# Projection products of the last sections as two row halves, with one ring of seven PSUM banks

## The chip, the cores and the metric

The kernel runs on one core of a Trainium2 chip. Five engines work side by side, each through its own queue in order: TensorE (PE) multiplies matrices into PSUM, VectorE (DVE) and ScalarE (ACT) read PSUM, GpSimd (POOL) works on SBUF, and SyncE (SP) issues most DMAs. PSUM has eight banks; one holds a tile of 128 partitions by 512 fp32. The metric is the device time of one execution in microseconds, the median over several runs.

## The reference, cut to what matters

Two branches of one input x (2048 tokens, 512 features) are mixed by a gate per token:

```python
g = sigmoid((x * gate_w).sum(-1))
a = Re(DFT_seq(DFT_hidden(x)))                 # four matrix products with cos/sin matrices
q, k, v = heads(x @ wqkv)                      # 32 heads of 16
p = softmax(q @ k.T * 16 ** -0.5)              # full 2048 x 2048 per head
b = concat_heads(p @ v) @ wo                   # the projection
out = g * a + (1 - g) * b
```

The change concerns the projection with `wo` and the scores of the last head pair.

## The kernel before, in words

Matrix products keep fp32 accuracy by splitting an operand into a high and a low part of a reduced fp32 type: one product becomes three, high x high, high x low, low x high.

Heads are worked in 16 pairs. For a pair p, the 2048 queries are taken in two halves of 1024, and the keys in 16 tiles of 128: a *unit* u is one pair, one half and one key tile, 512 units in all. In a unit, `scores` makes four score tiles (two query blocks, two heads), each with the keys of 128 positions as stationary operand and 512 queries moving. Head 0 lies on rows 0 to 49 of the operands and head 1 on rows 64 to 113, so the scores of the two heads use different row halves of the PE array. Fifty rows hold the three split products and the row of maxima that makes the exponent safe. The maxima come from a second, transposed score tile (`a_tile`) that DVE reduces. ACT takes the exponential of each score tile from PSUM into `pt` (line 775); four value products per unit (`pv`, `pv_last`), each in its own 32 columns of the array, add into the bank `acc`.

Most of the kernel interleaves, by patterns written out by hand, one score or maximum on one row half with one product of the Fourier branch or the projection on the other row half (`segment`). When the maxima are done, the last ten *sections*, the loop at line 994, follow: u = 492, 494, to 510, two units each. A section issues, in this order on PE, four scores (two starts of two), the projection products that the table `whole` gives it, four more scores, and the eight value products of two earlier units (16 records in the profile). In 506, `turn` follows the products: four small products with the matrix `pairsum`, by which the last pair's sums and outputs are turned. In 508 `back`, one transpose, follows them. Both use all 128 rows.

A projection *chain* (`Chain`) is the sum of several products of 128 rows for one output tile t of 128 tokens in one PSUM bank: nine products over the head blocks 0 to 2 (generator `first`), or three for one block (`third`, `last`, `early`). When a chain's last product is issued, `proj_next` calls `finish`, which has DVE compute y = y + (1 - g) * PSUM (line 649) and, for the last block of the first token half, sends y out.

The eight banks are: `acc`; `psD` ("d") with one bank; and six banks in two rings of three, `psS` ("s", banks 0 to 2) and `psA` ("a", banks 3 to 5). A ring gives the bank that was touched least recently; a tile's first product waits until the last reader of the tile before it in that bank is done. In the last sections the scores of head 0 use ring s, those of head 1 ring a. Chains use d and s in turn, in 508 and 510 a, d and s. Ahead of section 492 stand four extra scores of head 1, in banks s, s, a and d.

After the sections, `products` makes the last pair's own projection for four output tiles, then come the last value products and `last_pair` with the end of the work.

Of the kernel before, what the change touches and what calls it, by code (L numbers as in the profile page):

```python
# [9 lines left out]
F32 = mybir.dt.float32  # L10
# [5 lines left out]
P = 128  # L16
# [15 lines left out]
def mix_kernel(ctx: ExitStack, tc: tile.TileContext, xa_t, xa, wqkv, w_hid, w_seq, wo, gate_w, out):  # L32
# [5 lines left out]
    nc = tc.nc  # L38
    ctx.enter_context(tc.manual_schedule())

    six = [ctx.enter_context(tc.tile_pool(name=f"ps{i}", bufs=1, space=PSUM)) for i in range(6)]

    used = list(range(6))

    class Ring:


        def __init__(self, *banks):
            self.banks, self.of = banks, {}

        def tile(self, shape, dtype, name, bank=None):
            i = min(self.banks, key=used.index) if bank is None else bank
            t = six[i].tile(shape, dtype, name=name, tag="t")
            self.touch(i)
            self.of[id(t)] = (t, i)
            return t
# [7 lines left out]
            if id(t) in self.of:  # L64
                self.touch(self.of[id(t)][1])

    psS, psA = Ring(0, 1, 2), Ring(3, 4, 5)
    psO = ctx.enter_context(tc.tile_pool(name="psO", bufs=1, space=PSUM))
    psD = ctx.enter_context(tc.tile_pool(name="psD", bufs=1, space=PSUM))
    dram = ctx.enter_context(tc.tile_pool(name="dram", bufs=1, space=DRAM))  # L70
# [114 lines left out]
    def bank():  # L185
        nonlocal banks
        banks += 1
        return (psS if banks % 2 else psA).tile([P, 512], F32, name="s" if banks % 2 else "a")


    with tc.tile_pool(name="qk", bufs=1, reuse_waits="tile") as pool:
# [38 lines left out]
        for tb in range(4):  # L230
# [4 lines left out]
            for c in range(2):  # L235
                if tb == 0 and c == 0:
                    pss = [bank() for _ in range(4)]
                    for kt in range(KT):
                        x = xab[tb][:, :, :, kt * P:(kt + 1) * P]
                        for i, (w, v) in enumerate(((wh, 0), (wl, 0), (wh, 1))):  # L240
                            for ct in range(4):
                                nc.tensor.matmul(pss[ct], w[:, c, kt, ct * P:(ct + 1) * P], x[:, :, v],
                                                 start=kt == 0 and i == 0, stop=kt == KT - 1 and i == 2)
# [4 lines left out]
                for ct in range(4):  # L248
                    ps = bank()
# [143 lines left out]
    for s in range(8):  # L393
        ps = psS.tile([P, 512], F32, name="s")
# [45 lines left out]
    class Chain:  # L440


        def __init__(self, pool, name, n):
            self.pool, self.name, self.left = pool, name, n
            self.begun = False

        def mm(self, st, mv, half, stop):
            if not self.begun:
                self.ps = self.pool.tile([P, 512], F32, name=self.name)
            r = slice(None) if half is None else slice(64 * half, 64 * half + 64)  # L450
            i = nc.tensor.matmul(self.ps, st[r], mv[r], start=not self.begun, stop=stop)  # L451
            self.begun = True
            return i

    def real():

        for s, t in enumerate(ab):
            chain = Chain(*((psA, "a") if s in (0, 2) else (psD, "d")), 12)
            for kt in range(KT):
                h1, l1 = (t[:, v, kt * P:(kt + 1) * P] for v in range(2))  # L460
                yield chain, h1, wre[0][kt], None
                yield chain, h1, wre[1][kt], None
                yield chain, l1, wre[0][kt], partial(real_next, s, t, chain) if kt == KT - 1 else None
# [58 lines left out]
    oh, yp, wos = {}, {}, []  # L522
# [115 lines left out]
    maxima_left = True  # L638

    def finish(ps, t, y, other=False):  # L640
        for ring in (psS, psA):
            ring.read(ps)
        if other:

            tmp = few
            nc.scalar.activation(tmp, ps, AF.Copy, scale=omg[:, t:t + 1])  # L646
            nc.gpsimd.tensor_tensor(y, y, tmp, ALU.add)  # L647
            return
        nc.vector.scalar_tensor_tensor(y, ps, omg[:, t:t + 1], y, op0=ALU.mult, op1=ALU.add)

    def proj(hf, cts, pools, qts=range(8)):

        for qt in qts:
            t = hf * 8 + qt
            chain = Chain(*pools[qt % len(pools)], 3 * len(cts))
            for ct in cts:
                h1, l1 = oh[hf, ct][qt]
                for i, (st, mv) in enumerate(((h1, 0), (h1, 1), (l1, 0))):
                    last = ct == cts[-1] and i == 2
                    yield chain, st, wos[0][:, mv, ct], partial(proj_next, hf, cts, t, chain) if last else None  # L660

    def proj_next(hf, cts, t, chain):
        finish(chain.ps, t, yp[t], maxima_left)
        if hf == 0 and cts[-1] == 3:
            nc.sync.dma_start(out[t * P:(t + 1) * P, :], yp[t])

# [22 lines left out]
    class LastPair:  # L689
# [35 lines left out]
        def products(self, pools, order, others=()):  # L725

            pss = [pool.tile([P, 512], F32, name=name) for pool, name in pools]
            for i, (st, mv) in enumerate(((0, 0), (0, 1), (1, 0))):
                for c in range(4):
                    r = slice(32 * c, 32 * c + 32)  # L730
                    nc.tensor.matmul(pss[c], self.o15[r, st], w15[0][r, mv], start=i == 0, stop=i == 2)
            for c in order:
                t = 8 + 4 * self.blk + c
                y = yp.pop(t)
                finish(pss[c], t, y, c in others)
                (nc.scalar if c in others else nc.sync).dma_start(out[t * P:(t + 1) * P, :], y)
# [3 lines left out]
    def last_pair(fill):  # L740
        x = LastPair(1, [(psS, "s")])
        x.copy(4)
        pump(fill, 1)
        x.turn()
        pump(fill, 4)
        x.back()
        drain(fill)
        x.products([(psA, "a")] * 3 + [(psD, "d")], (1, 2, 0, 3), (0,))
# [12 lines left out]
    def scores(u, qb, h, bank=(psS, "s"), number=None):  # L761
        p, r = divmod(u, 32)
        hf, kt = divmod(r, 16)
        q0 = hf * 1024 + qb * 512
        if u >= UNITS - 16:

            blk, kt = divmod(kt, 8)
            q0, kt = 1024 + blk * 512, 2 * kt + qb
        if u not in pts:
            pts[u] = work.tile([P, 4, 512], F32, name="pt", bufs=4)  # L770
        pool, name = bank
        ps = pool.tile([P, 512], F32, name=name) if number is None else pool.tile([P, 512], F32, name, number)
        rr = slice(64 * h, 64 * h + 50)
        nc.tensor.matmul(ps, ks[p % 2][rr, kt * P:(kt + 1) * P], qs[p % 2][rr, q0:q0 + 512], start=True, stop=True)  # L774
        return nc.scalar.activation(pts[u][:, 2 * qb + h], ps, AF.Exp, bias=0.0, scale=DH ** -0.5)  # L775
# [33 lines left out]
    def take(gen, n, whole=True):  # L809

        got = []
        while len(got) < n:
            x = next(gen, None)
            if x is None:
                break
            x[0].left -= 1
            got.append((*x, x[0].left == 0))
            if whole and got[-1][4]:
                break
        return got  # L820

    def issue(x, half, stop=True):
        chain, st, mv, after, last = x
        i = chain.mm(st, mv, half, last and stop)
        if stop and after:
            after()
        return i

    def pump(gen, n):
        for x in take(gen, n, False):  # L830
            issue(x, None)

    def drain(gen):
        while xs := take(gen, 9):
            for x in xs:
                issue(x, None)
# [6 lines left out]
    for hf in range(2):  # L843
        for ct in range(4):
            n = 3 if hf and ct == 3 else 4
            last = 32 * (4 * ct + n - 1) + 16 * (hf + 1)
# [9 lines left out]
    one, two, three = [(psD, "d")], [(psS, "s"), (psD, "d")], [(psS, "s"), (psA, "a"), (psD, "d")]  # L856
# [9 lines left out]
    def run_plan(u):  # L866
        for v in sorted(v for v in plan if v <= u + 1):
            for f in plan.pop(v):
                f()
# [31 lines left out]
    def values(full=False):  # L901
        nonlocal valued
        i = pv(valued, full)
        valued += 1
        return i
# [56 lines left out]
    first = proj(0, (0, 1, 2), one * 5 + two[:1] + one, range(7))  # L962
# [21 lines left out]
    for bank in (*three[:1], *three):  # L984
# [3 lines left out]
    third = proj(1, (3,), two)  # L988
    last = proj(0, (3,), three[1:] + three[:1], range(7))

    early, late = proj(0, (0,), one, (7,)), proj(0, (1, 2, 3), [(psS, "s")], (7,))
    whole = {492: ((first, 9),), 494: ((first, 6),), 496: ((first, 3), (third, 3)), 498: ((third, 6),), 500: ((third, 6),),
             502: ((third, 3),), 504: ((early, 3), (third, 3)), 506: ((third, 3),), 508: ((last, 9),), 510: ((last, 12),)}
    for u in range(valued + 2, UNITS, 2):
        run_plan(u)
        for i in range(4):
            if i == 2:
                for gen, n in whole[u]:
                    pump(gen, n)
                if u == 506:  # L1000
                    last_pairs[0].turn()
                elif u == 508:
                    last_pairs[0].back()
            for h in range(2):
                scores(u + i // 2, i % 2, h, three[h])
        values()
        values()
    last_pairs[0].products([(psS, "s"), (psA, "a"), (psA, "a"), (psD, "d")], range(4))
# [39 lines left out]
```

## Time and profile before

| what | value |
|---|---|
| runs | 1698.32, 1698.53, 1698.54 us; median 1698.53 |
| span of the profiled execution, first to last instruction | 1696.8 us |
| busy share of the span | PE 100%, DVE 81%, ACT 67%, POOL 26% |
| the ten sections, first score of 492 to last value product of 510 | 1633.1 to 1683.4 us of the span |
| in 1633.1 to 1681.5 us | PE 48.4 busy, ACT 42.2, DVE 17.9 of 48.4 us |
| granted PE clock | 1.00 up to 1680 us |

The page gives the profiled execution's span and no other time for it. Rows of the timeline have the start in us from the span's start, the length in us, the engine, the source line, the operation, output<-input and shapes, the count of merged instructions, and in brackets the idle time before with what ended it. The end of a matrix product is modelled: its start is the surer number. Lengths of neighbouring products overlap, since they are pipelined.

### The profile page before, as it was taken

What the parts mean: (1) busy time and instruction counts of PE and PEld (TensorE: products, weight loads), DVE (VectorE), ACT (ScalarE), POOL (GpSimd) and SP (SyncE); (2) the same over time, 40 slices, a digit from 0 to 9 for tenths busy, and PEclk for the clock granted to TensorE, in tenths of its full rate; (3) what the DMA queues carried; (4) which work ended last, traced back from release to release, by engine and by line L of the source; (5) the groups of instructions that cost most, each with busy time, mean ns of one, the idle gap of its engine ahead of it and who ended that gap; (6) DMA issues with size and microseconds to landing.
All of it is one profiled execution on the core that took longest, in us unless ns stands there. A gap on an engine that the chain in (4) does not pass through costs nothing.

```text
span 1696.8 us, 33721 instructions
## 1 busy us (share of the span) xinstructions
PE 1689.2 (100%) x13040; PEld 1076.1 (63%) x13040; DVE 1366.7 (81%) x2313; ACT 1138.6 (67%) x2242; POOL 449.6 (26%) x554
## 2 busy tenths in 40 slices
PE   9999999999999999999999999999999999999998
PEld 7888855556666666666666666666666666655544
DVE  5439888888888888888888888888888888889854
ACT  5212377777766777666777677776667776678886
POOL 0101122322222333222222343322323343211110
PEclk9999999999999999999999999999999999999999
DMA  8963600314141434314156435224141535362114
GB/s 294 344 146 132 161 8 13 47 39 76 57 76 46 88 98 97 73 39 82 38 95 243 96 108 109 68 63 77 50 83 58 120 111 101 129 187 39 36 30 138
DMA packets 82274, 165.10 MB, mean 97 GB/s; under 512 B 19460, under 2 KB 19954, under 8 KB 78274
## 3 DMA queue, kind: packets, MB, share of 16 engines
q1 hardware_dynamic: 77874, 161.99, 37.1%
q8 instruction: 103, 1.69, 0.4%
q0 software_dynamic: 3808, 0.30, 0.2%
q10 hardware_dynamic: 432, 0.66, 0.1%
q14 instruction: 57, 0.47, 0.1%
HBM read 107.73 MB, written 54.52 MB: 96 GB/s over the span
## 4 chain that ended last, share of the span: by engine, by line
PE 99%; DMA 0%; DVE 0%; DVEq 0%; ACT 0%; SPq 0%; issue 0%
PE d L451 33%; PE acc L796 27%; PE s L774 14%; PE a L284 12%; PE s L365 3%; PE s L397 1%; PE d L365 1%; PE acc L782 1%; PE a L106 1%; PE s L107 1%; PE a L107 1%; PE s L106 1%; PE s L105 1%; PE a L105 1%; PE s L451 1%; PE a L451 0%
## 5 line engine op out<-in xcount | busy, mean ns | idle before, releaser
L286 DVE TENSOR_REDUCE mx<-a 128x1 f32<-128x512 f32 x2026 | 1239.9, 681 | 213.1 <-PE a L284 199.1
L775 ACT ACTIVATE pt<-s 128x512 f32<-128x512 f32 x2006 | 1023.2, 620 | 403.0 <-PE s L774 390.5
L774 PE MATMUL s<-qs,ks 50*128 50x512 f32 x2006 | 794.0, 422 | 0.0
L284 PE MATMUL a<-ks,qs 48*128 48x512 f32 x2026 | 744.5, 398 | 0.0
L451 PE MATMUL d<-xab,ch 64*128 64x512 f32 x2016 | 647.8, 396 | 0.0
L774 PEld LDWEIGHTS s<-qs,ks 50*128 50x128 f32 x2006 | 365.4, 185 | 228.5 <-issue 177.5
L796 PE MATMUL acc<-pt,vt 128*17 128x512 f32 x3968 | 484.2, 596 | 0.0
L284 PEld LDWEIGHTS a<-ks,qs 48*128 48x128 f32 x2026 | 370.3, 186 | 53.2 <-DVE mx L286 23.2
L451 PE MATMUL d<-xab,cl 64*128 64x512 f32 x1008 | 399.4, 396 | 0.0
L451 PEld LDWEIGHTS d<-xab,ch 64*128 64x128 f32 x2016 | 366.7, 184 | 21.6
L435 POOL CAST ch<-craw 128x512 fp32r<-128x512 f32 x126 | 77.1, 612 | 549.1 <-PE a L284 282.2
L796 PEld LDWEIGHTS acc<-pt,vt 128*17 128x17 f32 x3968 | 102.3, 96 | 184.7 <-issue 184.5
L451 PEld LDWEIGHTS d<-xab,cl 64*128 64x128 f32 x1008 | 185.7, 184 | 10.5
L436 POOL TENSOR_TENSOR cl<-craw,ch 128x512 fp32r<-128x512 f32 x126 | 162.1, 1287 | 10.2
L309 POOL DMA_DIRECT2D qs<-mt x119 | 67.0, 568 | 150.3 <-DVE mt L303 147.8
L451 PE MATMUL d<-wre,xab 64*128 64x512 f32 x336 | 90.5, 402 | 0.0
L451 PEld LDWEIGHTS d<-wre,xab 64*128 64x128 f32 x336 | 59.0, 185 | 38.4 <-issue 23.3
L451 PE MATMUL d<-wo_hl,o_hl 64*128 64x512 f32 (+1 forms) x246 | 68.1, 409 | 0.0
L451 PEld LDWEIGHTS d<-wo_hl,o_hl 64*128 64x128 f32 (+1 forms) x246 | 42.3, 185 | 29.5 <-issue 12.1
L101 ACT CAST hl<-s 128x512 fp32r<-128x512 f32 x28 | 16.1, 587 | 58.5 <-PE s L365 31.4
L647 POOL TENSOR_TENSOR yp<-yp,few 128x512 f32<-128x512 f32 x12 | 15.4, 1283 | 112.4 <-ACT few L646 112.4
L469 POOL CAST xab<-y 128x512 fp32r<-128x512 f32 x16 | 9.8, 611 | 127.8 <-ACT y L467 99.6
(168 smaller groups left out, 1009.6 us busy)
## 6 DMA issues: line engine op xcount, KB each, us to landing
craw<-w_seq SPq DMA_DIRECT2D x128, 256.0 KB
qk<-hl SPq DMA_DIRECT2D x32, 512.0 KB
qs<-qk SPq DMA_DIRECT2D x96, 128.0 KB
ks<-qk SPq DMA_DIRECT2D x96, 128.0 KB
b<-hl SPq DMA_DIRECT2D x16, 512.0 KB
xab<-b SPq DMA_DIRECT2D x16, 512.0 KB
o<-oe SPq DMA_DIRECT2D x62, 128.0 KB
oh<-nh SPq DMA_DIRECT2D x12, 512.0 KB
```

The source lines that it names most:

```text
L105: nc.tensor.matmul(ps, sh, mh, start=first, stop=False)
L106: nc.tensor.matmul(ps, sh, ml, start=False, stop=False)
L284: nc.tensor.matmul(ps, qs[p % 2][r, qt * P:(qt + 1) * P], ks[p % 2][r, kb * 512:(kb + 1) * 512], start=True, stop=True)
L286: user = nc.vector.tensor_reduce(mx[p % 2][:, h, qt, kb:kb + 1], ps, AX.X, ALU.max)
L309: (nc.gpsimd if own else nc.sync).dma_start(rows.rearrange("v (q b c) -> v b q c", q=8, b=4)[:, b], mt[hf][32 * b + h:32 * b + 32:2])
L365: i = nc.tensor.matmul(ps, st[r], mv[r], start=not half and not j, stop=half == 1 and j == 11)
L435: nc.gpsimd.tensor_copy(h1, raw)
L436: nc.gpsimd.tensor_tensor(l1, raw, h1.bitcast(F32), ALU.subtract)
L451: i = nc.tensor.matmul(self.ps, st[r], mv[r], start=not self.begun, stop=stop)
L774: nc.tensor.matmul(ps, ks[p % 2][rr, kt * P:(kt + 1) * P], qs[p % 2][rr, q0:q0 + 512], start=True, stop=True)
L775: return nc.scalar.activation(pts[u][:, 2 * qb + h], ps, AF.Exp, bias=0.0, scale=DH ** -0.5)
L796: i = nc.tensor.matmul(acc[32 * j:32 * j + 17], vt[:, kt, p, 16 * h:16 * h + 17], pt[:, j], start=kt == 0, stop=kt == NT - 1)
```

## The change

`used`, the order of touches, now covers seven banks, the seventh being the one of `psD`, and a third ring `psAll` holds all seven. `Chain` gets a method `both`, which issues a product as two of 64 rows, rows 0 to 63 into one bank and rows 64 to 127 into another. The last sections call `halves` instead of `pump`, so that every chain there uses two banks, whatever pool it was made with. `proj_next` finishes both banks, one after the other, into the same y. The scores of the sections take their banks from `psAll` as well. The table `whole` moves three products of `first` from 496 to 494. The code behind the sections (`products`, `last_pair`, `turn`, `back`) and everything before them stays.

```diff
-    used = list(range(6))
+    used = list(range(7))
...
-            t = six[i].tile(shape, dtype, name=name, tag="t")
+            t = (psD.tile(shape, dtype, name="d") if i == 6 else
+                 six[i].tile(shape, dtype, name=name, tag="t"))
...
-    psS, psA = Ring(0, 1, 2), Ring(3, 4, 5)
+    psS, psA, psAll = Ring(0, 1, 2), Ring(3, 4, 5), Ring(*range(7))
...
-            self.begun = False
+            self.begun, self.other = False, None
...
+        def both(self, st, mv, stop):
+            if not self.begun:
+                self.ps, self.other = (psAll.tile([P, 512], F32, n) for n in "sa")
+            for half, ps in enumerate((self.ps, self.other)):
+                r = slice(64 * half, 64 * half + 64)
+                nc.tensor.matmul(ps, st[r], mv[r], start=not self.begun, stop=stop)
+            self.begun = True
...
-        for ring in (psS, psA):
+        for ring in (psS, psA, psAll):
             ring.read(ps)
...
         finish(chain.ps, t, yp[t], maxima_left)
+        if chain.other is not None:
+            finish(chain.other, t, yp[t])
...
+    def halves(gen, n):
+        for chain, st, mv, after, last in take(gen, n, False):
+            chain.both(st, mv, last)
+            if after:
+                after()
...
-    whole = {492: ((first, 9),), 494: ((first, 6),), 496: ((first, 3), (third, 3)), 498: ((third, 6),), 500: ((third, 6),),
+    whole = {492: ((first, 9),), 494: ((first, 9),), 496: ((third, 3),), 498: ((third, 6),), 500: ((third, 6),),
              502: ((third, 3),), 504: ((early, 3), (third, 3)), 506: ((third, 3),), 508: ((last, 9),), 510: ((last, 12),)}
...
-                    pump(gen, n)
+                    halves(gen, n)
...
-                scores(u + i // 2, i % 2, h, three[h])
+                scores(u + i // 2, i % 2, h, (psAll, "sa"[h]))
```

## The prediction

> **What bounds the kernel now.** I read the page first, and in it the chain that ended last.
>
> ```profile
> PE 99%; DMA 0%; DVE 0%; DVEq 0%; ACT 0%; SPq 0%; issue 0%
> ```
>
> TensorE (PE) carries 99% of the chain, so time goes or comes where PE's own order gets shorter or waits. The change touches only the ten sections u = 492 to 510 near the end. I cut them out of the timeline at the first score of each. In the PE timeline this is the section u = 500 (the rows into bank a, which start with those into s, are left out); below it, from ScalarE's (ACT's) timeline, the exponentials of its first four scores:
>
> ```profile
> 1653.19 0.49 PE L774 MATMUL s<-qs,ks 50*128 50x512 f32 x1
> ...
> 1653.52 0.39 PE L774 MATMUL s<-qs,ks 50*128 50x512 f32 x1
> ...
> 1653.85 0.96 PE L451 MATMUL d<-wo_hl,o_lno 128*128 128x512 f32 x3
> 1654.65 0.87 PE L451 MATMUL s<-wo_hl,o_lnh 128*128 128x512 f32 x3
> 1655.44 0.50 PE L774 MATMUL s<-qs,ks 50*128 50x512 f32 x1
> ...
> 1655.78 0.39 PE L774 MATMUL s<-qs,ks 50*128 50x512 f32 x1
> ...
> 1656.11 1.91 PE L782 MATMUL acc<-pt,vt 128*17 128x512 f32 x16
> 1657.95 0.50 PE L774 MATMUL s<-qs,ks 50*128 50x512 f32 x1
> ```
>
> ```profile
> 1653.78 0.60 ACT L775 ACTIVATE pt<-s 128x512 f32<-128x512 f32 x1 [0.50 <-PE a L774]
> 1654.27 0.59 ACT L775 ACTIVATE pt<-a 128x512 f32<-128x512 f32 x1
> 1654.75 0.61 ACT L775 ACTIVATE pt<-s 128x512 f32<-128x512 f32 x1
> 1655.22 0.62 ACT L775 ACTIVATE pt<-a 128x512 f32<-128x512 f32 x1
> ```
>
> I number the eight scores S1 to S8 (S1 with S2, S3 with S4 and so on start together, on rows 0 and 64). The starts give the prices. From S1 to S3 0.33 us; S3 to products 0.33; first chain of three 0.80; second 0.79; S5 to S7 0.34; S7 to value products 0.33; these 1.84. Sum 4.76. Nothing waits in between: the section is PE's own pace. The exponentials of S1 to S4 start 0.59, 1.08, 1.56 and 2.03 after S1 and end at 1.19, 1.67, 2.17 and 2.65.
>
> The stretches, section by section (columns: length, then busy time of PE, weight loads, VectorE, ACT, GpSimd), for u = 502 (one chain), 508 (three), and 510 (four):
>
> ```profile
> 1657.95:1662.01 4.06, 4.06 (x31) 1.51 (x28) 0.75 (x1) 3.56 (x9) 0.00 (x0) 1.00 0.32 74
> 1671.67:1677.22 5.55, 5.55 (x39) 2.72 (x36) 2.32 (x4) 4.35 (x10) 0.00 (x0) 1.00 0.38 142
> 1677.22:1683.37 6.15, 6.15 (x40) 3.14 (x36) 2.83 (x4) 4.12 (x9) 0.00 (x0) 1.00 0.44 171
> ```
>
> One chain less makes 4.76 into 4.06: three products cost 0.70, 0.233 each, when no mode change is counted.
>
> **The change, part by part.** *Products as two halves.* 66 products of 128 rows become 132 of 64 rows. The DFT stage shows what such pairs cost:
>
> ```profile
> 1000.69 0.39 PE L451 MATMUL d<-xab,ch 64*128 64x512 f32 x1
> 1000.71 0.40 PE L774 MATMUL s<-qs,ks 50*128 50x512 f32 x1
> 1000.92 0.39 PE L451 MATMUL d<-xab,cl 64*128 64x512 f32 x1
> ```
>
> A 64-row product and a score start 0.02 apart and the next pair comes 0.23 later, so a pair costs what one 128-row product costs: nothing added, weight loads included. If the halves ran in turn it would be 66 x 0.233 = 15.4 more; that is the upper end and becomes a rival.
>
> *Mode changes gone.* The scores use row halves, the products now too. The excess of the quoted gaps over 0.233 is 0.10 (S3 to products), 0.80 - 0.70 = 0.10 (first chain), 0.79 - 0.70 = 0.09 (last chain) and 0.10 (S5 to S7): about 0.40 per section. It goes in eight sections. In 506 and 508 the small products of turn() and back(), on 128 rows, follow the chains, so the change of mode is moved behind the chains and nothing goes. Gain if nothing waits: 8 x 0.40 = 3.2 us. That is all there is to win. A section then runs S1 at 0, S3 at 0.335, products at 0.57, S5 after 0.70 per chain, S7 0.23 later, value products 0.32 after that, next S1 1.84 later.
>
> *Second halves read out.* Each of 18 chains leaves a second bank, so VectorE (DVE) gets 18 more multiply-adds into the same rows of y. Their prices:
>
> ```profile
> 1679.59 0.75 DVE L649 SCALAR_TENSOR_TENSOR yp_qs<-d,omg,yp_qs 128x512 f32<-128x512 f32 x1
> 1680.29 0.75 DVE L649 SCALAR_TENSOR_TENSOR yp_qs<-s,omg,yp_qs 128x512 f32<-128x512 f32 x1
> ```
>
> ```profile
> 1637.19 0.42 DVE L610 CAST o_lno<-o_raw 128x512 fp32r<-128x512 f32 x1
> 1637.64 0.69 DVE L611 TENSOR_TENSOR o_lno<-o_raw,o_lno 128x512 fp32r<-128x512 f32 x1
> ```
>
> Independent ones start 0.69 to 0.70 apart. The second of a chain reads what the first wrote; such a pair (the cast, then the subtraction) starts 0.03 after the first has ended, so 0.75 + 0.03 = 0.78. A chain takes 0.78 + 0.69 = 1.47 of DVE instead of 0.69. DVE is idle most of this stretch, so I cost the work at nothing where one or two chains stand in a section; in 508 and 510 it holds banks, below.
>
> *One ring of seven.* Banks are taken strictly in rotation, so each tile waits for the reader of the tile seven before it. With 8 + 2k tiles per section (k chains) S7 and S8 reach back as follows. k = 2: S6 to S3, S7 to S4. k = 1: S7 to S2, S8 to S3. Before, two rings of three and the chains' own bank let S7 reach back to S1 and S8 to S2, whose exponentials were long over. How fast PE follows a release, and what a stalled product costs besides, this earlier place shows (a score that waits, its neighbour, then value products):
>
> ```profile
> 1607.10 0.49 PE L774 MATMUL s<-qs,ks 50*128 50x512 f32 x1
> 1607.17 0.39 PE L284 MATMUL a<-ks,qs 48*128 48x512 f32 x1
> 1607.52 1.05 PE L796 MATMUL acc<-pt,vt 128*17 128x512 f32 x8
> ```
>
> The waiting score takes 0.49 instead of 0.39 and the value products follow 0.42 after it, not 0.32: a stall refills the pipe for 0.10. PE follows ACT's end by about 0.06, from the first section, PE and then ACT:
>
> ```profile
> 1633.13 0.50 PE L774 MATMUL s<-qs,ks 50*128 50x512 f32 x1
> 1633.28 0.39 PE L774 MATMUL d<-qs,ks 50*128 50x512 f32 x1
> ...
> 1634.15 2.33 PE L451 MATMUL s<-wo_hl,o_hl 128*128 128x512 f32 x9
> ...
> 1638.92 0.49 PE L774 MATMUL s<-qs,ks 50*128 50x512 f32 x1
> ```
>
> ```profile
> 1633.51 0.59 ACT L775 ACTIVATE pt<-s 128x512 f32<-128x512 f32 x1
> 1633.98 0.61 ACT L775 ACTIVATE pt<-a 128x512 f32<-128x512 f32 x1
> 1634.46 0.62 ACT L775 ACTIVATE pt<-d 128x512 f32<-128x512 f32 x1
> ```
>
> The chain's first product at 1634.15 starts 0.05 after the exponential that read its bank ended (1633.51 + 0.59).
>
> Now the sum, section by section, as change of length. Where a wait decides, I write when PE could start and when it may.
>
> - 492: S1 is given the old d bank, whose extra score (1633.28) is only read at 1634.46 to 1635.08. So S1 starts at 1635.14, not 1633.13; nine products from 1635.71, S5 at 1637.80, value products at 1638.35, next S1 at 1640.20, before 1638.92: **+1.28**. Everything on PE queues behind this wait, and ACT runs dry until 1635.7 (S1 + 0.59).
> - 494: no wait; two mode changes less: **-0.40**. (Its three products more are taken from 496: no change.)
> - 496 and 502, k = 1: S7 and S8 could start at 1.50; S8 waits for S3's exponential, 2.17 + 0.06 = 2.23. Value products at 2.23 + 0.42 = 2.65, end 4.49 against 4.06: **+0.43 each**.
> - 498, 500, 504, k = 2 (all three some 4.76 long before, as the quoted 500): S7 could start at 2.20; S4's exponential allows 2.71. Value products at 3.13, end 4.97 against 4.76: **+0.21 each**.
> - 506: the same wait on S4, mostly covered by turn(), an estimate: **+0.1**.
> - 508, k = 3: the third chain waits for S3 (1.97 to 2.23). S7 and S8 take the second chain's banks. DVE reads at 1.46 (0.57, two more products of 0.233, 0.39 for the last to land and 0.04 for DVE to follow), 2.24, 2.93, 3.71; the last ends at 4.46, so S8 starts at 4.52, value products 4.94, end 6.78 against 5.55: **+1.23**.
> - 510, k = 4: S8 takes the third chain's first bank, read at 4.40 to 5.15: S8 at 5.21, end 7.47 against 6.15: **+1.32**.
>
> Sum: 1.28 - 0.40 + 0.86 + 0.63 + 0.1 + 1.23 + 1.32 = +5.0 us. The last second half of 510 is read by 7.40, just ahead of the products that follow at 7.47, so the tail after it keeps its length. The profiled span of 1696.8 becomes 1701.8. The runs' median, 1698.53, stands 1.7 above the span; with the same distance I predict 1703.5 us, 0.29% slower. 0.2%, 3.4 us, is about what a measurement of this kernel can tell from no change.
>
> Bounds. Without the refill of 0.10 in the eight waiting sections the sum is +4.2. If the second read of a chain started 0.69 after the first, 508 and 510 would gain back some 0.2 each. If each mode change were worth nothing, it would be up to 1 more, no more, since the waits are set by ACT and DVE and only 492 and 494 run free.
>
> **The rivals.** *Waits covered.* All depends on PE reaching S7 before S4 (or S3) has been read. If ACT's readers were done about 0.7 earlier, or S7's bank came from further back, only the mode changes would count: 1698.53 - 3.2 = 1695.3, or 1696.6 with the stall of 492 left in. For it: ACT is busy 3.56 of 4.06 in 502, so it has slack on average. Against: the slack lies after the value products, and the offsets 2.17 and 2.65 do not move with PE. [...]
>
> *Half the waits.* If the exponentials are handed over sooner, because scores without a change of mode before them land 0.1 earlier (0.39 long rather than 0.50), or DVE chains its pairs tighter, 508 and 510 cost about half (-1.3) and the others lose the refill (-0.6): +3.1, 1701.6, inside 0.2%.
>
> *Halves in turn.* If two halves on different rows with the same moving tile ran one after the other: +15.4, less the waits that this time would cover and the mode changes, so about +12: 1710. Against it: the quoted pairs, and nothing in the rows ties their speed to different moving tiles.
>
> **How the numbers follow.** Forecast 0.70; half the waits 0.20; waits covered 0.07; halves in turn 0.03. The predicted time is the first's. Range 1700.0 to 1705.5: from below the half case up to the forecast with mode changes worth nothing and a little more; the outer cases are left out, about 0.1 and some of the forecast's own spread. Faster by over 0.2% only if the covered case had more to win than I count: 0.03. Within 0.2%: the rest of that case and most of the half case, and a little of the forecast: 0.23. Slower: 0.74.
>
> **What would show it.** The profile after should have S1 of 492 start about 2 us later and wait for ACT; products following scores 0.23 after them, not 0.33; sections 502 at about 4.5 and 500 at about 5.0, with weight loads of L785 waiting for ACT; 508 and 510 about 1.2 longer, waiting for DVE L658; chain pairs on DVE 0.78 apart. I am wrong if the scores S7 and S8 do not wait, or if products in halves are spaced by more than 0.25.

## The result, and the profile after

The changed kernel takes 1705.41 us (median of four runs, 1703.83 to 1707.61); the kernel before takes 1698.53 (1698.32 to 1698.78). The ratio is 1.0041 with a 95% interval of 1.0029 to 1.0053: slower by 0.41%, 6.9 us. The profiled execution took 1705.32 us with a span of 1703.5, 6.7 more than before. Two things were foreseen too small or not at all: the size (5.0 us), and that the runs now differ by 3.8 us where they differed by 0.5. The 0.5 is of four runs; in the 22 and 29 runs of the kernel before that were made beside the experiments, its time spread over 1.4 and 1.8 us.

The first line below is the head of the page of the kernel after, the second the chain that ended last. TensorE (PE) still carries 99% of the chain, and its busy share went only from 100% to 99%. An average says nothing of where 6.7 us came from, so the stretches have to be read.

```profile
PE 1694.0 (99%) x13106; PEld 1076.1 (63%) x13106; DVE 1380.9 (81%) x2331; ACT 1138.6 (67%) x2242; POOL 449.5 (26%) x554
...
PE 99%; DVE 0%; ACT 0%; issue 0%; DVEq 0%; ACTq 0%
```

Cut at the first scores of the sections, as in the prediction, the ten sections changed as follows. Section 492 is taken from the start of the extra scores ahead of it (1632.47 before, 1632.31 after).

| section | length before | after | change | predicted change |
|---|---|---|---|---|
| 492, with the extra scores | 6.45 | 9.24 | +2.79 | +1.28 |
| 494 (three products more) | 4.74 | 5.03 | +0.29 | +0.30 (-0.40, +0.70) |
| 496 (three products fewer) | 4.76 | 4.43 | -0.33 | -0.27 (+0.43, -0.70) |
| 498, 500, 504 | 14.29 | 14.92 | +0.63 | +0.63 |
| 502 | 4.06 | 4.49 | +0.43 | +0.43 |
| 506 | 4.90 | 5.01 | +0.11 | +0.1 |
| 508 | 5.55 | 6.92 | +1.37 | +1.23 |
| 510 | 6.15 | 7.57 | +1.42 | +1.32 |
| sum | 50.90 | 57.61 | +6.71 | +5.0 |

*The middle sections.* PE's timeline of section 500 of the kernel after, without some of the rows of the second row half. The `s` and `a` of a row are now only the names of tiles: the new ring can put either into any of its banks.

```profile
1656.02 0.50 PE L785 MATMUL d<-qs,ks 50*128 50x512 f32 x1
...
1656.36 0.39 PE L785 MATMUL s<-qs,ks 50*128 50x512 f32 x1
...
1656.59 0.40 PE L461 MATMUL s<-wo_hl,o_lno 64*128 64x512 f32 x1
1656.60 0.40 PE L461 MATMUL a<-wo_hl,o_lno 64*128 64x512 f32 x1
1656.83 0.40 PE L461 MATMUL s<-wo_hl,o_lno 64*128 64x512 f32 x1
...
1658.01 0.39 PE L785 MATMUL s<-qs,ks 50*128 50x512 f32 x1
1658.24 0.50 PE L785 MATMUL a<-qs,ks 50*128 50x512 f32 x1
1658.73 0.49 PE L785 MATMUL s<-qs,ks 50*128 50x512 f32 x1
...
1659.16 1.91 PE L793 MATMUL acc<-pt,vt 128*17 128x512 f32 x16
1661.00 0.49 PE L785 MATMUL s<-qs,ks 50*128 50x512 f32 x1
```

The change does what it says: two halves start 0.01 apart, the next pair 0.24 later, and products follow the scores after 0.23 (1656.36 to 1656.59) where it was 0.33. But S7 starts 0.72 after S5, not 0.23. ScalarE's (ACT's) timeline shows what it waited for, the exponentials of S1, S3 and S4:

```profile
1656.61 0.60 ACT L786 ACTIVATE pt<-d 128x512 f32<-128x512 f32 x1 [0.95 <-PE a L785]
...
1657.58 0.61 ACT L786 ACTIVATE pt<-s 128x512 f32<-128x512 f32 x1
1658.06 0.62 ACT L786 ACTIVATE pt<-a 128x512 f32<-128x512 f32 x1
```

The fourth exponential ends at 1658.68 and S7 starts 0.05 later, as on record. S6 starts at 1658.24, 0.05 after the third has ended at 1658.19: the reach of the new ring is the foreseen one, S6 to S3 and S7 to S4.

*Section 492.* PE's timeline, again of the kernel after, and then its 1-us stretches (columns: length, busy time of PE, weight loads, VectorE, ACT, GpSimd; then the granted clock, DMA share and GB/s):

```profile
1633.12 0.39 PE L785 MATMUL d<-qs,ks 50*128 50x512 f32 x1
1634.96 0.79 PE L785 MATMUL d<-qs,ks 50*128 50x512 f32 x1 [1.46 <-ACT pt L786]
...
1635.98 0.62 PE L461 MATMUL s<-wo_hl,o_hl 64*128 64x512 f32 x1
...
1636.41 0.62 PE L461 MATMUL s<-wo_hl,o_hl 64*128 64x512 f32 x1
...
1639.15 0.39 PE L785 MATMUL s<-qs,ks 50*128 50x512 f32 x1
...
1641.55 0.50 PE L785 MATMUL s<-qs,ks 50*128 50x512 f32 x1
```

```profile
1634.00:1635.00 1.00, 0.04 (x2) 0.04 (x2) 0.00 (x0) 0.91 (x2) 1.00 (x1) 0.96 0.00 0
1635.00:1636.00 1.00, 1.00 (x6) 0.81 (x8) 0.00 (x0) 0.21 (x1) 1.00 (x1) 0.50 0.01 2
1636.00:1637.00 1.00, 1.00 (x8) 0.81 (x6) 0.00 (x0) 1.00 (x3) 0.22 (x1) 0.50 0.03 4
1637.00:1638.00 1.00, 1.00 (x8) 0.81 (x6) 0.00 (x0) 0.86 (x2) 0.00 (x0) 0.50 0.01 2
1638.00:1639.00 1.00, 1.00 (x10) 0.79 (x10) 0.00 (x0) 0.00 (x0) 0.00 (x0) 0.83 0.03 4
```

S1 waits for the old d bank as foreseen: 1.46 us with nothing on PE. What follows was not foreseen. The granted clock is 0.50 from the end of that wait on, for 3.42 us, an estimate from the stretches that takes it as either 1.00 or 0.50: a stretch of 1 us at 0.96 holds 0.08 at half clock, one at 0.83 holds 0.34, and three full ones lie between. Meanwhile products take 0.62 and stand 0.43 apart, in place of 0.39 and 0.23. From S1 to the next section's S1 it is 6.59 us; the prediction had 5.06.

*Sections 508 and 510.* VectorE's (DVE's) timeline of the kernel after, in 508:

```profile
1676.90 0.75 DVE L658 SCALAR_TENSOR_TENSOR yp<-d,omg,yp 128x512 f32<-128x512 f32 x1 [1.99 <-PE a L461]
1677.76 0.75 DVE L658 SCALAR_TENSOR_TENSOR yp<-a,omg,yp 128x512 f32<-128x512 f32 x1
1678.43 0.74 DVE L658 SCALAR_TENSOR_TENSOR yp<-s,omg,yp 128x512 f32<-128x512 f32 x1
```

The second read of a chain starts 0.86 after the first, and the next chain's first 0.67 after that. PE's waits in 1630 to 1690 us name DVE behind three scores, one in 508 and two in 510 (columns: total us, times, longest):

```profile
PE a L785 <- DVE yp L658: 0.4, 1, 0.4
PE s L785 <- DVE yp_qs L658: 0.4, 1, 0.4
PE a L785 <- DVE yp_qs L658: 0.2, 1, 0.2
```

### The profile page after: what moved, and what is told of

The parts are those of the page before. It is cut to its first block, busy times and chain, and to the rows that moved or that the text cites. A ratio compares the mean times of both kernels' runs of the same rounds, so it can differ in the third digit from the quotient of the medians.

```text
span 1703.5 us, 33887 instructions
## 1 busy us (share of the span) xinstructions
PE 1694.0 (99%) x13106; PEld 1076.1 (63%) x13106; DVE 1380.9 (81%) x2331; ACT 1138.6 (67%) x2242; POOL 449.5 (26%) x554
## 4 chain that ended last, share of the span: by engine, by line
PE 99%; DVE 0%; ACT 0%; issue 0%; DVEq 0%; ACTq 0%
PE d L452 33%; PE acc L807 27%; PE s L785 13%; PE a L285 12%; PE s L366 3%; PE s L398 1%; PE d L366 1%; PE acc L793 1%; PE a L108 1%; PE a L107 1%; PE s L108 1%; PE s L107 1%; PE a L106 1%; PE s L106 1%; PE s L461 0%; PE s L243 0%
## 5 line engine op out<-in xcount | busy, mean ns | idle before, releaser
L452 PE MATMUL d<-wo_hl,o_hl 64*128 64x512 f32 x234 | 64.5, 408 | 0.0
L452 PEld LDWEIGHTS d<-wo_hl,o_hl 64*128 64x128 f32 x234 | 40.2, 184 | 28.0 <-issue 11.1
```

## The experiments

Theory A is the prediction's: three kinds of bank waits (the d bank in 492, exponentials in the middle, DVE in 508 and 510). It needed one addition, that PE's idle time in 492 lowers the clock. Rival B says that the wait alone costs what it lasts and that the slow products come from something else: the pairs themselves, or the place in the execution.

### e1_touch: the stall of 492 taken away

The d bank is marked as the latest touched before the loop, so that it comes last in the rotation. Against the kernel after:

```diff
+    psAll.touch(6)
     for u in range(valued + 2, UNITS, 2):
```

> The changed kernel with one line more: the d bank counts as just used when the last sections begin, so the first score of 492 gets a bank that has long been read. Theory (the wait for the d bank makes PE idle, the idle time makes the granted clock fall to 0.50 for some 3 us): 492 has no long idle time, the clock stays at 1.00; 2.8 us go (1.3 of waiting, 1.5 of slow clock), 0.3 come back because the chain's second bank is read late: about 1702.9 us, and the runs agree within 0.5 us again. Rival (the clock falls because of the paired products, not because of the idle time): the clock is 0.50 in 492 here too, only the wait goes: about 1704.3 us. All other sections as in the changed kernel.

Measured: 1703.68 us (1703.08 to 1704.0, six runs), 1.0029 of the kernel before with an interval of 1.0018 to 1.0041. In 492 PE never stands idle, the clock stays at 1.00 and the next section's S1 comes 6.76 after the extra scores, not 9.24: 2.48 saved, more than the wait of 1.46. Only the chain's second bank comes late there, as expected: 6.76 is 0.31 above the 6.45 of before. The runs agree within 0.9 us, where 0.5 was expected. One stretch of e1_touch, from its 492:

```profile
1635.00:1636.00 1.00, 1.00 (x12) 0.81 (x10) 0.00 (x0) 1.00 (x4) 1.00 (x1) 1.00 0.01 2
```

The total is 0.8 above theory A's, and its trace says why. With another rotation, turn() in 506 gets a bank that is still being read. PE's waits of e1_touch:

```profile
PE s L723 <- ACT pt L786: 0.8, 1, 0.8
```

Section 506 lasts 5.80 (1668.06 to 1673.86) where it lasted 5.01. That is the 0.8. The clock stayed at 1.00 after this shorter wait.

### e2_stall: the stall alone, in the kernel before

Only the first score of 492 takes the d bank; no halves, no new ring. Against the kernel before:

```diff
-                scores(u + i // 2, i % 2, h, three[h])
+                scores(u + i // 2, i % 2, h, (psD, "d") if u == 492 and not i and not h else three[h])
```

> The kernel before with one edit: the first score of 492 takes the d bank. Theory: the same wait (some 2 us later start) and the same fall of the clock without any paired product: 1.3 + 1.5 us, about 1701.3 us, runs spread by over 1 us. Rival (the clock has to do with the pairs): only the wait, 1699.8 us, clock 1.00 from 1635 on.

Measured: 1701.06 us (1699.34 to 1702.13, eleven runs), ratio 1.0013 with an interval of 1.0004 to 1.0022. The median is theory A's within 0.25, but the runs fall into two groups: five at 1699.34 to 1700.21, near the rival's 1699.8, and six at 1701.06 to 1702.13, among them the one with the trace (1701.61). PE's timeline of e2_stall, and its stretches:

```profile
1635.02 0.49 PE L774 MATMUL d<-qs,ks 50*128 50x512 f32 x1 [1.46 <-ACT pt L775]
...
1635.68 3.86 PE L451 MATMUL s<-wo_hl,o_hl 128*128 128x512 f32 x9
```

```profile
1635.00:1636.00 1.00, 0.98 (x5) 0.60 (x6) 0.00 (x0) 0.45 (x1) 1.00 (x1) 1.00 0.01 2
1636.00:1637.00 1.00, 1.00 (x4) 0.79 (x3) 0.00 (x0) 1.00 (x4) 0.38 (x1) 0.56 0.03 4
1637.00:1638.00 1.00, 1.00 (x3) 0.76 (x3) 0.00 (x0) 0.61 (x2) 0.00 (x0) 0.50 0.01 2
1638.00:1639.00 1.00, 1.00 (x4) 0.66 (x2) 0.00 (x0) 0.00 (x0) 0.00 (x0) 0.50 0.03 4
1639.00:1640.00 1.00, 1.00 (x6) 0.31 (x4) 0.43 (x1) 0.00 (x0) 0.00 (x0) 0.73 0.01 2
```

The same idle time, and about 1 us after its end the same half clock, again for 3.42 us (0.88 + 1 + 1 + 0.54). The nine whole products take 3.86 instead of the 2.33 that the prediction showed of before: 1.53 more. No product is paired here, so the pairs are not the cause. The mean clock of the five faster runs is 0.999, that of five of the six others 0.998: the clock may not have fallen in each execution, and none of the faster five has a trace.

### e7_warm: the stall kept, PE not idle in it

Eight products into a spare bank are put ahead of the loop. They compute nothing that is used. Against the kernel after:

```diff
+    if True:
+        t = psAll.tile([P, 512], F32, "a", 4)
+        for _ in range(8):
+            nc.tensor.matmul(t, ks[1][0:50, 0:P], qs[1][0:50, 0:512], start=True, stop=True)
```

> The changed kernel with eight score-like products into an idle bank ahead of section 492, which are read by nobody: PE works while the first score waits for the d bank. Theory: the wait stays (score at about the same time), the clock stays at 1.00, so only the slow clock's 1.5 us go: about 1703.9 us, runs within 0.5 us. Rival (clock falls by the pairs): 1705.4 us as the changed kernel, clock 0.50 after the wait.

Measured: 1708.19 us (1708.55, 1708.32, 1705.16, 1704.89, 1708.19), ratio 1.0047. As a total it is a miss for both theories. PE's timeline of e7_warm in 492, then in 506, and stretches of both:

```profile
1635.46 0.50 PE L785 MATMUL d<-qs,ks 50*128 50x512 f32 x1 [0.30 <-ACT pt L786]
...
1640.50 0.50 PE L785 MATMUL s<-qs,ks 50*128 50x512 f32 x1
...
1672.11 1.55 PE L723 MATMUL s<-pairsum,oe 128*128 128x64 f32 x8 [1.30 <-ACT pt L786]
...
1674.74 3.61 PE L793 MATMUL acc<-pt,vt 128*17 128x512 f32 x16
```

```profile
1635.00:1640.00 5.00, 4.70 (x43) 2.74 (x42) 1.58 (x3) 3.89 (x8) 1.90 (x1) 1.00 0.02 3
...
1672.00:1674.00 2.00, 1.89 (x10) 1.77 (x12) 1.69 (x5) 0.06 (x1) 0.00 (x0) 0.65 0.00 0
1674.00:1676.00 2.00, 2.00 (x12) 0.41 (x14) 0.29 (x2) 1.52 (x4) 0.00 (x0) 0.50 0.00 0
1676.00:1678.00 2.00, 2.00 (x12) 0.17 (x4) 0.00 (x0) 0.54 (x2) 0.00 (x0) 0.50 0.00 0
1678.00:1680.00 2.00, 2.00 (x14) 1.44 (x12) 0.00 (x0) 0.83 (x2) 0.00 (x0) 0.64 0.00 0
```

In 492 S1 starts just as late, but PE was idle only 0.30, the clock stays at 1.00, and S1 to the next S1 takes 5.04, which is the 5.06 of the prediction. From the extra scores on, 492 takes 7.69 instead of 9.24. So in these traces the clock, and with it 1.55 us, hangs on the idle time. The gain is lost in 506: the spare tile moved the rotation, turn() waits with PE idle for 1.30, the clock is 0.50 for 6.84 us (1.40 + 2 + 2 + 1.44), twice 3.42, and sixteen value products take 3.61 instead of 1.91. The same mechanism in another place, not foreseen.

### e3_ring: the ring of seven, without halves

Whole products, one bank per chain, every bank from the new ring. Against e1_touch:

```diff
-                self.ps, self.other = (psAll.tile([P, 512], F32, n) for n in "sa")
-            for half, ps in enumerate((self.ps, self.other)):
-                r = slice(64 * half, 64 * half + 64)
-                nc.tensor.matmul(ps, st[r], mv[r], start=not self.begun, stop=stop)
+                self.ps = psAll.tile([P, 512], F32, "s")
+            nc.tensor.matmul(self.ps, st, mv, start=not self.begun, stop=stop)
```

> The ring of seven alone: scores and chains take banks from it, with the line of e1, but products stay whole (128 rows, one bank per chain, one read). Theory (waits come from the second banks, which bring a tile's bank back two exponentials sooner): no waits, mode changes as before: 1698.5 us, at most 0.4 off; section of 500 about 4.76 long. Rival (the ring itself makes scores wait): sections longer than before, 1700 us or more.

Measured: 1698.67 us (1698.22 to 1699.7, eleven runs), ratio 1.0001 with an interval of 0.9992 to 1.001. Once the first score of 492 is kept off the d bank, the ring by itself costs nothing. What e1_touch still loses comes from two banks per chain in it.

### e5_two: halves and ring only in 492 and 494

Those are the two sections that the prediction calls free, once the d bank is out of the way. Against e1_touch:

```diff
-                    halves(gen, n)
+                    (halves if u < 496 else pump)(gen, n)
...
-                scores(u + i // 2, i % 2, h, (psAll, "sa"[h]))
+                scores(u + i // 2, i % 2, h, (psAll, "sa"[h]) if u < 496 else three[h])
```

> As e1, but halves and ring only in 492 and 494; from 496 on whole products and the old rings. Theory: 494 gains 0.4 (two mode changes), 492 loses 0.3 (its chain waits for the late read of an extra score's bank): 1698.4 us. Rival (pairs cost more than whole products): over 1700 us.

Measured: 1698.89 us (1698.2 to 1699.4, eleven runs), ratio 1.0000 with an interval of 0.9991 to 1.0009. Pairs cost no more than whole products: 18 products with their halves in turn would have cost 18 x 0.233 = 4.2 us more. The total alone says little of the gain, since three small changes add up to +0.35 in its trace: against e3_ring, 492 takes 6.74 instead of 6.45 (the late bank), 494 5.06 instead of 5.43, and 496 4.50 instead of 4.07, where the old rings take over (a score that waits for an exponential would explain it; no row here shows it). The gain itself is clean in 494 of e1_touch: S1 to S5 takes 2.62 there (1639.18 to 1641.80) and 2.93 in e3_ring (1639.90 to 1642.83), with nine products in both. That is 0.31 less for three of the prediction's four excess gaps of 0.10; the whole section is 0.41 shorter (5.02 and 5.43), for its 0.40.

### e4_oneread: the second halves not read

Against e1_touch:

```diff
-            finish(chain.other, t, yp[t])
+            psAll.read(chain.other)
```

> As e1, but the second bank of a chain is read by nobody (the lower halves of the products of these sections are left out of y). Theory (508 and 510 wait for VectorE's second reads, the others for exponentials): 508 and 510 shorter by 1.0 and 1.5 us, all others unchanged: 2.5 us less than e1, about 1700.4 us. Rival (VectorE has slack, the waits of 508 and 510 are exponentials too): as e1, 1702.9 us.

Measured: 1701.17 us (1700.42 to 1701.58, eleven runs), 2.51 under e1_touch. DVE's timeline of e4_oneread in 510:

```profile
1680.67 2.28 DVE L658 SCALAR_TENSOR_TENSOR yp_qs<-s,omg,yp_qs 128x512 f32<-128x512 f32 x3 [3.28 <-PE a L461]
1682.93 0.75 DVE L658 SCALAR_TENSOR_TENSOR yp_qs<-d,omg,yp_qs 128x512 f32<-128x512 f32 x1
```

Four reads are over by 1683.68, where the kernel after needs eight. Section 508 lasts 5.87 instead of 6.92 in e1_touch, 510 lasts 6.12 instead of 7.57: 1.05 + 1.45 = 2.50, the whole difference. So both sections waited for the second reads. The eight other sections are as long as in e1_touch within 0.02, so their waits are not DVE's.

### e9_halfexp and e10_halfexp_before: the readers made faster

In e9_halfexp, on top of e4_oneread, the exponentials and the value products take 256 of 512 columns from unit 492 on, so the banks of the scores come free sooner. The kernel before with the same half work is e10_halfexp_before.

```diff
-        return nc.scalar.activation(pts[u][:, 2 * qb + h], ps, AF.Exp, bias=0.0, scale=DH ** -0.5)
+        cols = slice(0, 256 if u >= 492 else 512)
+        return nc.scalar.activation(pts[u][:, 2 * qb + h, cols], ps[:, cols], AF.Exp, bias=0.0, scale=DH ** -0.5)
...
-            i = nc.tensor.matmul(acc[32 * j:32 * j + 17], vt[:, kt, p, 16 * h:16 * h + 17], pt[:, j],
+            c = slice(0, 256 if u >= 492 else 512)
+            i = nc.tensor.matmul(acc[32 * j:32 * j + 17, c], vt[:, kt, p, 16 * h:16 * h + 17], pt[:, j, c],
```

> As e4, but from unit 492 on exponentials and value products take only the first 256 of 512 columns (half of that work is left out), so ACT's reads end far earlier; its partner is the kernel before with the same half work. Theory (late reads alone eat the gain): no waits left from 494 on, each section 0.4 shorter than the partner's, but in 506 and 508: partner - 2.5 us, about 1687.4 us if the partner is at 1689.9. Rival (mode changes are worth nothing, or pairs run slower): equal to the partner or slower.

> The kernel before with exponentials and value products of the units from 492 on over 256 of 512 columns (half of that work is left out). Nothing waited there before, so all theories expect only the shorter value products: 10 x 0.86 us less, about 1689.9 us.

Measured: 1693.83 us (1692.87 to 1694.74, seven runs) and 1695.80 (1693.72 to 1697.14, eleven runs). With faster readers, and without the second reads, the halves are 2.0 faster than the whole products, where 2.5 was expected. The level of e10_halfexp_before, 1689.9, is missed by 6. Shorter sections ran into waits for DVE, and the clock fell there also. PE's timeline of e10_halfexp_before, then its stretches:

```profile
1669.26 0.47 PE L774 MATMUL s<-qs,ks 50*128 50x512 f32 x1 [3.41 <-DVE on L716]
```

```profile
1670.00:1671.00 1.00, 1.00 (x3) 0.86 (x4) 0.00 (x0) 1.00 (x4) 0.00 (x0) 0.62 0.00 0
1671.00:1672.00 1.00, 1.00 (x4) 0.72 (x4) 0.64 (x1) 0.03 (x1) 0.00 (x0) 0.50 0.00 0
1672.00:1673.00 1.00, 1.00 (x4) 0.81 (x3) 0.47 (x2) 0.00 (x0) 0.00 (x0) 0.50 0.01 2
1673.00:1674.00 1.00, 1.00 (x6) 0.52 (x6) 0.52 (x2) 0.02 (x1) 0.00 (x0) 0.67 0.69 260
```

Again 3.42 us (0.76 + 1 + 1 + 0.66). In e9_halfexp a wait of 1.46 for DVE was followed by 0.50 as well (4 us at 0.57 from 1655 us on). A second wait of 1.23, which ended at 1668.83, was not: the clock stays at 1.00 up to the end of PE's work. This is the second among PE's waits of e9_halfexp, and below it a stretch of 1 us behind it:

```profile
PE s L785 <- DVE yp L658: 1.2, 1, 1.2
```

```profile
1670.00:1671.00 1.00, 1.00 (x12) 0.94 (x10) 0.37 (x1) 0.64 (x3) 0.00 (x0) 1.00 0.00 0
```

So the two totals hold different stalls, and their difference alone proves little. A clean section says more: 498 takes 3.68 in e9_halfexp (1646.12 to 1649.80) and 3.91 in e10_halfexp_before (1646.17 to 1650.08), 0.23 less although S8 still starts 0.07 after S7 (1648.39 and 1648.32). In the kernel after the same section is 0.24 longer than before. In this section, the sign of the change hangs on how early the banks are read.

One more idea has no run here: two chains at once, each half of either in the other's bank, so that a chain needs one bank. It would put both row halves into one bank at the same time, and nothing here shows whether that works or what it costs.

## Why the prediction was right, and where it was short

It was slower as foreseen, and inside the range. The forecast of 1703.5 stands 1.9 under the median, and each step can be placed.

- *Products as two halves, nothing added*: right. Pairs start 0.01 apart and 0.23 to 0.24 after each other, and in e5_two 18 such pairs cost nothing that shows in the total. The rival "halves in turn" falls.
- *Mode changes gone*: right in size, 0.10 for each gap (494 of e1_touch against e3_ring: 0.31 for three of them, 0.41 for the section; 0.23 between scores and products where it was 0.33).
- *The waits for exponentials* in 496 to 506: right within 0.06 in each section, though the +0.1 of 506 was an estimate without a working. S7 started 0.05 after the fourth exponential. The 0.10 behind a stall, on record as a refill, is in the rows as well: value products follow S7 by 0.43 (1658.73 to 1659.16) where it was 0.33 before (1655.78 to 1656.11). So "waits covered" and "half the waits" fall. e9_halfexp shows in one section that with faster readers the first comes true in part: 0.23 of 0.40.
- *508 and 510*: the mechanism is right (e4_oneread takes back 2.50), the size a little low. The step "such a pair starts 0.03 after the first has ended, so 0.78" took the price from a cast followed by a subtraction. Two multiply-adds into the same rows start 0.84 to 0.86 apart, so that two chains' reads end some 0.14 later than foreseen. 508 came out at +1.37 for +1.23 and 510 at +1.42 for +1.32.
- *492*: this term failed, +1.28 on record and +2.79 measured. S1 started where it was foreseen: 2.65 after the first extra score (1632.31 to 1634.96), foreseen 2.67. What was mis-sized is the step behind it, "nine products from 1635.71, S5 at 1637.80". It priced them with the rows of a PE that had not stood still. After 1.46 of idleness the clock was 0.50, and 6.59 instead of 5.06 passed until the next section. e2_stall's trace shows that the wait alone brings it, e7_warm's that PE's being busy in the wait takes it away.

The sections exceed the sum by 1.7: 1.5 in 492, 0.24 in 508 and 510, less some hundredths in the others. The stretch ahead of them is 0.16 shorter and the tail 0.15 longer. On record the tail kept its length, with the last second half of 510 read by 7.40 after S1. It was read at 7.61, and the products behind the section took 1.06 where they took 0.90 before and in e4_oneread, which leaves that read out. The other 0.2 of the median's 1.9 is its distance from the profiled span, 1.9 where it was 1.7.

Apart from the 0.10 behind a stall, the prediction's bounds and cases were what each wait lasts; none had a slower clock behind a wait. Its upper end of 1705.5 held by 0.1, and that was luck: the room above the forecast was meant for mode changes worth nothing "and a little more", and one of the four runs took 1707.61.

No version that does the whole work beat the kernel before. e3_ring and e5_two equal it. What there is to win, 0.4 us in a section that doesn't wait, is small against the waits that two banks per chain bring.

## What to carry to other kernels

Before a tile is given a second bank, lay the rotation out for a few steps, with the time at which each bank's reader is done: each extra bank shortens the reach of the ring by one tile, and it was that reach which hid the readers. Price a new wait on PE with what may follow it: behind 1.46 us of idleness came another 1.5 us of slow products in the traces of after and e2_stall, behind 1.23 us in e9_halfexp nothing. And when an edit moves a rotation, every later user of a bank is moved, also those that it doesn't touch: turn() lost in e1_touch 0.8 us and in e7_warm more than the gain.

## What the runs showed of the hardware that was not expected

PE's standing idle for 1.30 (e7_warm), 1.46 (after, e2_stall, e9_halfexp) and 3.41 us (e10_halfexp_before) was followed, at once or up to about 1.4 us later (e9_halfexp), by a granted clock of 0.50. Idle times of 0.55 (e10_halfexp_before), 0.82 (e1_touch) and 1.23 us (e9_halfexp) were not. The low phase lasted 3.42 us in after, e2_stall and e10_halfexp_before, and 6.84 in e7_warm.

So 1.30 us of idleness was enough in e7_warm, and 1.23 us was not in e9_halfexp. Whether the two enclose a fixed limit stays open, and so does why the low phase lasted twice as long in e7_warm.

The runs of the kernels that stall spread (after: 1703.83 at a mean clock of 0.999, 1.5 below the run with the trace, and 1707.61 at 0.997; the two groups of e2_stall; e7_warm: two runs at 1704.9 and 1705.2 with 1.000 and 0.999, three at 1708.2 to 1708.6 with 0.997 and 0.998). That one and the same stall lowers the clock for a different time in each execution, or in some not at all, would fit this spread. It is argued only: one execution of each kernel has a trace.
